# Where a step computes the scores of an attention tail and the product with U

## The chip, the cores and the metric

The kernel runs on one core of a Trainium2 chip. The metric is the time of one execution on the device in microseconds (us), the median of several executions. A profiled execution adds a trace: the start and end of every instruction on the engines PE (matrix products; PEld is its loading of weights), DVE (vector), ACT (scalar), POOL and SP, what each waited for, and every DMA.

## The reference

Everything is float32. For each of 8 batches and 8 heads there are 576 rows of queries, keys and values, 64 wide. Each row of scores keeps its 32 largest entries:

```
scores = q @ k.T / sqrt(64)              # 576 x 576 for each head
kth    = the 32nd largest of each row
attn   = softmax(where(scores >= kth, scores, -1e9))
x      = attn @ v                        # heads side by side: 8 x 576 x 512
h      = x.T @ U @ V                     # U 576 x 32, V 32 x 576: mixes the 576 rows
u      = x + h.T
out    = u + relu(u @ w_ch1) @ w_ch2     # 512 -> 2048 -> 512
```

## The kernel before

**Pairs and steps.** Two heads are one pair (`g`, 32 of them, 4 in a batch). The 576 rows of a pair are four tiles of 128 rows (`t` = 0 to 3) and a tail of 64 rows (`t` = 4, `NT`). A tile holds both heads side by side. The tail's 64 rows of one head lie on partitions 0 to 63 and those of the other on 64 to 127, so that the two heads' tails fill one tile. The list `steps` gives the first four pairs five steps each. From pair 4 on a pair has four steps, and the last of them holds two items, tile 3 and the tail: `steps += [[(g, t)] for t in range(NT - 1)] + [[(g, NT - 1), (g, NT)]]`. There are 132 steps.

**The pipeline.** The main loop counts `n` over the steps, and in one turn it works on several of them. It starts with the weighted sums of values of step n-3 (`weighted`, which calls `values`), goes on to the scores of step n+1 (`scores`, `fold`), turns the probabilities of steps n-1 and n-2 for use as a matmul operand (`turned`, `blocks`, `back`), and between these moves the top-32 search of step n (`front`) forward on DVE. `fill` is called eight times in a turn. Each call advances the generator `mixed` by one stage if one is in `mixing`, and then issues matmuls of the channel MLP of an earlier batch (`mlp`, lines 707 and 725) until a share `due` is used up. Nothing is reordered later: every engine runs its instructions in the order in which this loop issues them.

**Scores.** `scores(g, t)` multiplies queries by keys, 64 deep, into PSUM tiles `sc` (two of them, each two banks of 512 columns) and copies them to SBUF with ACT (line 361, or 368 to 370 for the first pairs). A tile takes two PSUM tiles, 288 of 512 columns in each bank, and four products of 288 columns. Each head uses one half of the PE's rows and all 128 columns (64\*128 in the trace). From pair 5 on (`blocked`) DVE later reads the first of the two PSUM tiles once more (`split`, line 400), to fold the row in two by a maximum. The tail has its own branch (`if t == NT`, lines 343 to 353): one PSUM tile, four products with 288 columns for the two heads (five where the keys of one head are stored in a rotated order), each in one quarter of the PE (64\*64), and one ACT copy into `Stail` (line 352). From pair 4 on the loop calls it at the end of the turn before the one that scores tile 3 (lines 1210 and 1211). `Stail` is first read by DVE a turn and a half later (line 468).

**Values.** `values(g, t)` multiplies probabilities by values into a PSUM tile `O`: lines 616 and 619, the latter eight products that use half of the PE's columns each (128\*64). For a tail it is line 603. ACT copies `O` into `XT` (line 628).

**The mixing with U and V.** When the tail of a pair is done, `weighted` puts `mixed(g, 5, 1 ...)` into `mixing`. One `fill` later this turns `XT` into `X` (line 642, an ACT copy, and a division by the softmax sums on POOL, line 647), then lets five `fill`s pass. The product with U follows: five products that use a quarter of the PE's columns each (line 653, `pT`, 128\*32), copied by ACT into `Tb` (line 661). The next two `fill`s multiply by V and add X (lines 665 and 667, `up`) into `uT`, the input of the MLP. With a batch's fourth pair the MLP of that batch is put into the queue `fillers`. The MLP of the last batch (`closing`, line 801) runs when all else is done.

Of the kernel before, what the change touches and what calls it, by code (L numbers as in the profile page):

```python
# [8 lines left out]
F32 = mybir.dt.float32  # L9
# [17 lines left out]
def kernel(  # L27
# [28 lines left out]
    nc = tc.nc  # L56
    B, H, S, D = q.shape
    P = 128
# [4 lines left out]
    NT, TAIL = 4, 64  # L63
    MAIN = NT * P
    HALF = S // 2
    assert S == MAIN + TAIL and D == 64 and H % 2 == 0 and C == 512 and TOPK % 8 == 0
    NPAIR = H // 2
# [15 lines left out]
    attn = ctx.enter_context(tc.tile_pool(name="attn", bufs=2))  # L83
# [43 lines left out]
    def rows(t):  # L127
        return P if t < NT else TAIL

    def cols(t):  # L130
        return slice(t * P, t * P + rows(t))
# [4 lines left out]
    def half(h):  # L136
        return slice(h * D, (h + 1) * D)
# [97 lines left out]
    raw, qkTs, S2s, uTs, XTs, dens = {}, {}, {}, {}, {}, {}  # L235
    probs, PTs, folds, fronts_of = {}, {}, {}, {}
# [54 lines left out]
    def blocked(g):  # L291

        return g > NPAIR
# [23 lines left out]
            copy(qkT[:, i, 0:MAIN], tp.rearrange("p t n -> p (t n)"))  # L319
            yield  # L320

    def scores(g, t):

        qkT = qkTs[g]
        if t == NT and g >= NPAIR:
            S2 = attn.tile([P, S], F32, tag="Stail", name="Stail", bufs=1)
        else:
            S2 = attn.tile([P, 2 * (S + TAIL)], F32, tag="Ssb", name="Ssb", bufs=4)  # L330
        n = 2 if t < NT else 1
        probs[g, t] = S2
        S2s[g, t] = S2[:, 0 : n * S].rearrange("p (c n) -> p c n", c=n)
        def product(out, h, lo, hi):
            nc.tensor.matmul(  # L335
                out,
                lhsT=qkT[half(h), 0, cols(t)],
                rhs=qkT[half(h), 1, lo:hi],
                start=True,
                stop=True,  # L340
            )

        if t == NT:
            sc = ps_s.tile([P, 2, 512], F32, tag="sc", name="sc")
            for i in range(2):
                for h in range(2):
                    lo = i * HALF + (TAIL if h and blocked(g) else 0)
                    hi = min(lo + HALF, S)
                    product(sc[half(h), i, 0 : hi - lo], h, lo, hi)
                    if hi - lo < HALF:  # L350
                        product(sc[half(h), i, hi - lo : HALF], h, 0, TAIL)
            nc.scalar.copy(S2[:, 0:S].rearrange("p (i n) -> p i n", i=2), sc[:, :, 0:HALF])
            return
        scs = [ps_s.tile([P, 2, 512], F32, tag="sc", name="sc") for _ in range(2)]
        for i, sc in enumerate(scs):
            for h in range(2):
                part = 1 - i if h and blocked(g) else i
                product(sc[:, h, 0:HALF], h, part * HALF, (part + 1) * HALF)
        if blocked(g):
            for i, sc in enumerate(scs):  # L360
                nc.scalar.copy(ends_of(S2, i), sc[:, :, 0:HALF])  # L361
            fronts_of[g, t] = scs[0][:, :, 0:HALF]
            return

        main = S2.rearrange("p (h n) -> p h n", h=2)
        last = S2[:, MAIN : MAIN + 2 * TAIL].rearrange("p (h n) -> p h n", h=2)
        copy = nc.vector.tensor_copy if g + t == 0 else nc.scalar.copy
        copy(main[:, :, 0:HALF], scs[0][:, :, 0:HALF])  # L368
        nc.scalar.copy(main[:, :, HALF:MAIN], scs[1][:, :, 0 : MAIN - HALF])
        nc.scalar.copy(last, scs[1][:, :, MAIN - HALF : HALF])  # L370

    def ends_of(S2, i):

        parts = S2[:, 0 : 4 * HALF].rearrange("p (a n) -> p a n", a=4)
        return parts[:, 1:3] if i else parts[:, 0:4:3]
# [217 lines left out]
    def values(g, t):  # L593

        PT = PTs.pop((g, t))
        va, vd, vt = (a[g % NV] for a in (vas, vds, vts))
        O = ps_t.tile([P, P], F32, tag="tp", name="O")
        if t == NT:
            den, x = dens[g], xs[g % 2]
            if g not in inverted:  # L600
                inverse(g, 2 * NT if g == NPAIR - 1 else 0, 2 * NT + 1)
            for j in range(NT + 1):
                nc.tensor.matmul(  # L603
                    O,
                    lhsT=PT[:, j],
                    rhs=va[:, :, j, :] if j < NT else vt,
                    start=(j == 0),
                    stop=(j == NT),
                )
            for h in range(2):  # L610
                nc.scalar.mul(x[half(h), NT, half(h)], O[half(h), half(h)], den[half(h), 2 * NT :])
            return
        if shared(g, t):
            PT = PT.rearrange("p c n -> p (c n)")
            PT = PT.rearrange("p (a c j) -> p c a j", a=4, j=BLK)
        nc.tensor.matmul(O, lhsT=vd, rhs=PT[:, 2 * NT], start=True, stop=False)  # L616
        for j in range(NT):
            for h in range(2):
                nc.tensor.matmul(  # L619
                    O[half(h)],  # L620
                    lhsT=va[:, h, j, :],
                    rhs=PT[:, NT * h + j],
                    start=False,
                    stop=(j == NT - 1),
                )
        if t == 0:
            XTs[g] = attn.tile([P, MAIN], F32, tag="XT", name="XT", bufs=1)
        nc.scalar.copy(XTs[g][:, cols(t)], O)  # L628


    def mixed(g, wait, lag=0):

        for _ in range(lag):
            yield
        b, gi = divmod(g, NPAIR)
        if gi == 0:
            uTs[b] = mlpp.tile([P, NC, S], F32, tag="uT", name="uT")
        XT, den = XTs.pop(g), dens[g]
        X = xs[g % 2]
        tp = ps_t.tile([P, NT, P], F32, tag="tp", name="tp")  # L640
        for t in range(NT):
            nc.tensor.transpose(tp[:, t, :], XT[:, cols(t)], ident)
        X4 = X[:, 0:NT, :].rearrange("p t (h d) -> p t h d", h=2)
        tp4 = tp.rearrange("p t (h d) -> p t h d", h=2)
        den4 = den[:, 0 : 2 * NT].rearrange("p (t h) -> p t h ()", h=2).to_broadcast([P, NT, 2, D])
        nc.scalar.copy(X4, tp4)
        nc.gpsimd.tensor_tensor(X4, X4, den4, ALU.mult)
        for _ in range(wait):
            yield
        pT = ps_t.tile([P, P], F32, tag="tp", name="pT")  # L650
        for t in range(NT + 1):
            i = t % NT * R
            nc.tensor.matmul(
                pT[i : i + R, :],
                lhsT=U[:, t, :],
                rhs=X[:, t, :],
                start=(t < NT),
                stop=(0 < t),
            )
        Tb = mlpp.tile([P, P], F32, tag="Tb", name="Tb")  # L660
        nc.scalar.copy(Tb, pT)
        yield
        for chunks, (lo, hi) in zip(PARTS, SPAN):
            up = ps_t.tile([P, WIDE], F32, tag="tp", name="up")
            nc.tensor.matmul(up[:, 0 : hi - lo], lhsT=Tb, rhs=V[:, lo:hi], start=True, stop=False)  # L665
            for t in chunks:
                nc.tensor.matmul(  # L667
                    up[:, OFF[t] - lo : OFF[t] - lo + rows(t)],
                    lhsT=X[:, t, :],
                    rhs=ident if t < NT else ident2,  # L670
                    is_transpose=True if t < NT else None,
                    start=False,
                    stop=(t == chunks[-1]),
                )
            nc.scalar.copy(uTs[b][:, gi, lo:hi], up[:, 0 : hi - lo])
            yield
        if gi == NPAIR - 1:
            fillers.append(closing(b) if b == B - 1 else mlp(b))

    posts, ticks = [], 0  # L680

    def later(wait, job):

# [338 lines left out]
    STEPS = len(steps)  # L1022
# [5 lines left out]
    fillers, mixing, due = [], [], 0.0  # L1028
# [21 lines left out]
    def tiles(n):  # L1050

        return steps[n] if 0 <= n < STEPS else []

    def weighted(m):

        for g, t in reversed(tiles(m)):
            values(g, t)
        if tiles(m)[-1][1] == NT:
            mixing.append(mixed(g, 5, 1 if m < STEPS - 1 else 0))

    def turn():

# [10 lines left out]
    t = 0  # L1073
    for _ in prep(0):
        pass
    scores(0, 0)
    turning = ready = iter(())
    fronts = {}
    for n in range(STEPS + 2):
        if n < STEPS:  # L1080
            g, t = steps[n][0]
# [6 lines left out]
        else:  # L1088
            t = NT
# [71 lines left out]
        fill()  # L1161
        if ALONE <= n - 3 <= STEPS - 3:
            weighted(n - 3)
        for tile_ in tiles(n + 1):
            if tile_[1] < NT:
                scores(*tile_)
            fold(*tile_)
        turn()
        fill()
# [37 lines left out]
            next_params(1)  # L1207
        next(here, None)
        fill()
        if len(tiles(n + 2)) > 1:  # L1210
            scores(*tiles(n + 2)[1])
        fill()
    while mixing or fillers:
        fill()
# [33 lines left out]
```

## Time and profile before

| | |
|---|---|
| median of 3 executions | 1689.52 us (1689.05 to 1690.55) |
| profiled execution | 1690.17 us |
| its span, first to last instruction | 1688.4 us |
| PE busy | 1597.7 us (95%), 9328 matmuls |
| DVE busy | 1544.0 us (91%) |
| ACT busy | 1001.9 us (59%) |
| POOL busy | 938.1 us (56%) |
| PE in 500 to 1500 us | no idle time in the record |
| scores of a tail with 64 rows of the PE and 64 columns | 32 times, first at 35.6 us, last at 1513.2 us |
| product with U | 32 times, first at 87.1 us, last at 1563.9 us |

The span is 1.8 us below the profiled execution's own time and 1.1 us below the median. A float32 matmul of the program is two records in the trace, each with its load of weights. The record of a matmul [...]overlaps the next one, so the cost of a matmul is read from the distance between starts, not from its duration. Counts such as x10 are counts of records.

### The profile page before, as it was taken

The numbers are of one execution on the slowest core, as the hardware profiler recorded it, in microseconds if no ns is written. First come the engines' busy times: TensorE is split into PE (matmuls) and PEld (weight loads), VectorE is DVE, ScalarE is ACT, GpSimd is POOL, SyncE is SP. The second block draws the span as 40 slices with busy tenths as digits, with TensorE's granted clock in tenths as the row PEclk, the third lists the DMA queues.
The fourth block names the chain that finished last, engine by engine and source line by source line (L and its number), as shares of the span: only waits on it lengthen the run. The fifth ranks groups of instructions, "written<-read, shape, count | busy, mean of one in ns | idle before, by whom it ended". The sixth has DMA issues, their size and how long they took to land.

```text
span 1688.4 us, 29105 instructions
## 1 busy us (share of the span) xinstructions
PE 1597.7 (95%) x9328; PEld 1202.3 (71%) x9328; DVE 1544.0 (91%) x4364; ACT 1001.9 (59%) x2447; POOL 938.1 (56%) x741
## 2 busy tenths in 40 slices
PE   4667799999999999999999999999999999999999
PEld 2444566788677877778777887778777887778876
DVE  7999998999999999999999999999999999994452
ACT  4888778665555556565665556565655656564320
POOL 4778668655555555555555555555555555553620
PEclk7787798999999999999999999999999999999999
DMA  3323232254545545454444545454445455443001
GB/s 87 97 77 93 59 89 72 59 134 122 126 115 134 125 126 135 122 133 119 126 116 129 125 130 124 124 129 127 122 114 129 124 134 126 126 116 102 10 1 29
DMA packets 273897, 180.96 MB, mean 107 GB/s; under 512 B 171376, under 2 KB 258256, under 8 KB 273744
## 3 DMA queue, kind: packets, MB, share of 16 engines
q1 hardware_dynamic: 257712, 117.49, 30.1%
q10 hardware_dynamic: 16032, 61.61, 11.3%
q8 instruction: 74, 1.21, 0.3%
q14 instruction: 79, 0.65, 0.1%
HBM read 108.23 MB, written 70.78 MB: 106 GB/s over the span
## 4 chain that ended last, share of the span: by engine, by line
PE 82%; DVE 14%; ACT 1%; issue 1%; POOL 1%; DMA 1%; SPq 0%; ACTq 0%; DVEq 0%; POOLq 0%
PE mm L725 26%; PE mm L707 24%; PE sc L335 9%; PE O L619 7%; DVE m L486 6%; DVE upper L481 5%; PE mm L801 3%; PE up L665 2%; DVE first L468 2%; PE O L603 2%; PE tp L801 2%; PE sc L801 2%; PE O L616 1%; PE tp L578 1%; PE up L667 1%; PE tp L749 1%
## 5 line engine op out<-in xcount | busy, mean ns | idle before, releaser
L516 POOL TENSOR_TENSOR Ssb<-Ssb,E 128x576 f32<-128x576 f32 x243 | 339.6, 1417 | 273.7 <-ACT E L515 273.5
L707 PE MATMUL mm<-uT,w 128*128 128x320 f32 (+1 forms) x1792 | 468.7, 412 | 0.3 <-ACT hT L720 0.3
L725 PE MATMUL mm<-hT,w 128*128 128x320 f32 (+1 forms) x1792 | 468.0, 410 | 0.0
L707 PEld LDWEIGHTS mm<-uT,w 128*128 128x128 f32 x1792 | 331.6, 191 | 96.9 <-issue 9.0
L725 PEld LDWEIGHTS mm<-hT,w 128*128 128x128 f32 x1792 | 328.8, 190 | 90.7 <-issue 12.7
L486 DVE MAX8 m<-upper 128x8 f32<-128x304 f32 (+1 forms) x780 | 366.5, 510 | 0.7
L481 DVE MATCH_REPLACE8 upper<-m,upper 128x304 f32<-128x304 f32 (+1 forms) x520 | 259.3, 505 | 0.0
L398 POOL TENSOR_TENSOR lower<-Ssb 128x576 uint32<-128x576 uint32 x108 | 152.5, 1412 | 153.4 <-issue 102.2
L335 PE MATMUL sc<-qkT 64*128 64x288 f32 (+1 forms) x1334 | 213.1, 442 | 11.3 <-ACT Ssb L368 7.8
L405 ACT ACTIVATE Ssb<-Ssb,nmax 128x576 f32<-128x576 f32 x258 | 200.9, 780 | 17.4 <-POOL Ssb L492 9.2
L401 POOL TENSOR_TENSOR lower<-lower,upper 128x576 uint32<-128x576 uint32 x108 | 152.6, 1413 | 103.6 <-DVE upper L400 99.9
L453 DVE MAX8 upper<-lower 128x8 f32<-128x288 f32 x432 | 171.9, 438 | 9.8 <-POOL lower L401 9.7
L515 ACT ACTIVATE E<-Ssb,least 128x576 f32<-128x576 f32 x243 | 176.2, 768 | 4.3
L335 PEld LDWEIGHTS sc<-qkT 64*128 64x128 f32 (+1 forms) x1334 | 116.7, 184 | 74.5 <-issue 30.5
L542 DVE STREAM_TRANSPOSE y<-Ssb 128x512 f32<-128x512 f32 (+1 forms) x312 | 154.5, 544 | 7.0 <-ACT Ssb L405 6.4
L720 ACT ACTIVATE hT<-mm 128x320 f32<-128x320 f32 (+1 forms) x224 | 91.2, 407 | 100.8 <-PE mm L707 96.4
L361 ACT COPY Ssb<-sc 128x576 f32<-128x576 f32 x216 | 127.7, 644 | 37.0 <-PE sc L335 37.0
L619 PE MATMUL O<-PT,va 128*64 128x128 f32 x2048 | 145.1, 286 | 0.0
L619 PEld LDWEIGHTS O<-PT,va 128*64 128x64 f32 x2048 | 113.8, 141 | 16.4 <-issue 2.0
L400 DVE TENSOR_TENSOR upper<-sc,Ssb 128x576 f32<-128x576 f32 x108 | 80.1, 742 | 21.8 <-ACT Ssb L361 21.8
L628 ACT COPY XT<-O 128x128 f32<-128x128 f32 x128 | 33.9, 265 | 107.1 <-PE O L619 106.9
L481 DVE MATCH_REPLACE8 upper<-first,upper 128x304 f32<-128x304 f32 x216 | 97.4, 458 | 0.0
(247 smaller groups left out, 2191.6 us busy)
## 6 DMA issues: line engine op xcount, KB each, us to landing
away<-y SPq DMA_DIRECT2D x416, 144.0 KB, 2.5
PT<-away ACTq DMA_DIRECT2D x104, 576.0 KB, 3.8
raw<-in_moe_w_ch_dram SPq DMA_DIRECT2D x32, 512.0 KB, 3.8
va<-in_v_dram SPq DMA_DIRECT2D x64, 128.0 KB, 2.4
out_dram<-ob SPq DMA_DIRECT2D x59, 128.0 KB, 2.0
ld<-in_q_dram SPq DMA_DIRECT2D x108, 64.0 KB, 2.6
ld<-in_k_dram SPq DMA_DIRECT2D x108, 64.0 KB, 2.5
ld<-in_q_dram SPq DMA_DIRECT2D x108, 8.0 KB, 2.9
```

The lines of the kernel that those rows point to most:

```text
L335: nc.tensor.matmul(out, lhsT=qkT[half(h), 0, cols(t)], rhs=qkT[half(h), 1, lo:hi], start=True, stop=True,)
L401: nc.gpsimd.tensor_tensor(bottom, bottom, top.bitcast(U32), ALU.subtract)
L405: nc.scalar.activation(E, chunk, AF.Exp, bias=nmax, scale=SCALE, accum_out=total)
L453: nc.vector.max(spot, lower)
L481: nc.vector.match_replace(nxt, ms[c], curs[c], NEG)
L486: nc.vector.max(ms[c], curs[c])
L515: nc.scalar.activation(gap, chunk, AF.Relu, bias=least[:, c : c + 1], scale=-WIDEN)
L516: nc.gpsimd.tensor_tensor(chunk, chunk, gap, ALU.subtract)
L542: nc.vector.transpose(y[:, :, i * NT : i * NT + c].rearrange("p r c j -> p c r j"), E2[:, a : a + c * P].rearrange("p (c r j) -> p c r j", ...
L619: nc.tensor.matmul(O[half(h)], lhsT=va[:, h, j, :], rhs=PT[:, NT * h + j], start=False, stop=(j == NT - 1),)
L707: nc.tensor.matmul(ph[:, 0:w], lhsT=first_layer(cc, f), rhs=uT[:, cc, lo:hi], start=(cc == 0), stop=(cc == NC - 1),)
L725: nc.tensor.matmul(po[:, 0:w], lhsT=w2[:, f, c * P : (c + 1) * P], rhs=hTs[f][:, 0:w], start=(f == 0), stop=(f == NF - 1),)
```

## The change

Two pieces of work get other places in a turn, from pair 4 on.

The tail's scores are no longer computed at the end of a turn but by the call of `scores` that computes tile 3, ahead of tile 3's own products. They have no PSUM tile of their own: they go in three parts of 192 columns into columns 288 to 479 of three of the four banks that tile 3's scores use. The third part crosses the end of the first 512 keys and is computed in two pieces, so there are eight products (four of 192, two of 128, two of 64 columns). A new function copies them into `Stail` with two ACT copies (384 and 192 columns) after the copies of tile 3.

The product with U, for pairs 4 to 30, no longer follows after five `fill`s. `mixed` puts its pair into a new list `waiting` and stands still until the list is cleared. The main loop clears it in the next turn, right after the weighted values and ahead of the scores, and takes that one stage of `mixed` forward. The two stages with V follow at the next two `fill`s. The last pair keeps its five `fill`s. One variant of a buffer for tails of the first pairs is simplified and does the same as before.

```diff
-    def scores(g, t):
+    def scores(g, t, tail=False):
         qkT = qkTs[g]
-        if t == NT and g >= NPAIR:
-            S2 = attn.tile([P, S], F32, tag="Stail", name="Stail", bufs=1)
-        else:
-            S2 = attn.tile([P, 2 * (S + TAIL)], F32, tag="Ssb", name="Ssb", bufs=4)
+        S2 = attn.tile([P, 2 * (S + TAIL)], F32, tag="Ssb", name="Ssb", bufs=4)
...
         scs = [ps_s.tile([P, 2, 512], F32, tag="sc", name="sc") for _ in range(2)]
+        third = S // 3
+        spots = [sc[:, i, HALF : HALF + third] for sc, i in ((scs[0], 0), (scs[0], 1), (scs[1], 0))]
+        if tail:
+            rows_ = slice(MAIN, S)
+            for i, spot in enumerate(spots):
+                for h in range(2):
+                    lo, hi = i * third, min((i + 1) * third, MAIN)
+                    first_ = TAIL if h and blocked(g) else 0
+                    ranges = [(0, lo + first_, hi + first_)]
+                    if (i + 1) * third > MAIN:
+                        ranges.append((hi - lo, 0 if first_ else MAIN, TAIL if first_ else S))
+                    for to, lo, hi in ranges:
+                        nc.tensor.matmul(
+                            spot[half(h), to : to + hi - lo],
+                            lhsT=qkT[half(h), 0, rows_],
+                            rhs=qkT[half(h), 1, lo:hi],
+                            start=True,
+                            stop=True,
+                        )
...
             fronts_of[g, t] = scs[0][:, :, 0:HALF]
+            if tail:
+                tail_copies(g, scs, third)
             return
...
+    def tail_copies(g, scs, third):
+        S2 = attn.tile([P, S], F32, tag="Stail", name="Stail", bufs=1)
+        probs[g, NT] = S2
+        S2s[g, NT] = S2.rearrange("p (c n) -> p c n", c=1)
+        nc.scalar.copy(
+            S2[:, 0 : 2 * third].rearrange("p (i n) -> p i n", i=2), scs[0][:, :, HALF : HALF + third]
+        )
+        nc.scalar.copy(S2[:, 2 * third : S], scs[1][:, 0, HALF : HALF + third])
...
         nc.gpsimd.tensor_tensor(X4, X4, den4, ALU.mult)
-        for _ in range(wait):
-            yield
+        if wait is None:
+            waiting.append(g)
+            while g in waiting:
+                yield
+        else:
+            for _ in range(wait):
+                yield
         pT = ps_t.tile([P, P], F32, tag="tp", name="pT")
...
-            mixing.append(mixed(g, 5, 1 if m < STEPS - 1 else 0))
+            mixing.append(mixed(g, None, 1) if m < STEPS - 1 else mixed(g, 5, 0))
...
             weighted(n - 3)
+            if waiting:
+                waiting.clear()
+                if next(mixing[0], True):
+                    mixing.pop(0)
         for tile_ in tiles(n + 1):
             if tile_[1] < NT:
-                scores(*tile_)
+                scores(*tile_, len(tiles(n + 1)) > 1)
             fold(*tile_)
...
         fill()
-        if len(tiles(n + 2)) > 1:
-            scores(*tiles(n + 2)[1])
         fill()
```

More of the change, by code (lines that the diff above doesn't have):

```diff
@@ L370, in scores @@
         nc.scalar.copy(last, scs[1][:, :, MAIN - HALF : HALF])
+        if tail:
+            tail_copies(g, scs, third)
+    def tail_copies(g, scs, third):
[6 more added lines that the diff above has]
+        nc.scalar.copy(S2[:, 2 * third : S], scs[1][:, 0, HALF : HALF + third])
     def ends_of(S2, i):
@@ L678, in mixed @@
             fillers.append(closing(b) if b == B - 1 else mlp(b))
-    posts, ticks = [], 0
+    posts, ticks, waiting = [], 0, []
     def later(wait, job):
```

## The prediction

> **What bounds the kernel now.** I read the chain of work that ended last first. The line gives each engine's share of the span:
>
> ```profile
> PE 82%; DVE 14%; ACT 1%; issue 1%; POOL 1%; DMA 1%; SPq 0%; ACTq 0%; DVEq 0%; POOLq 0%
> ```
>
> PE carries the end. Where, is told by the busy times in stretches (columns: stretch, length, busy of PE, PEld, DVE, ACT, POOL with counts, granted PE clock, DMA share, GB/s):
>
> ```profile
> 432.00:1530.00 1098.00, 1097.66 (x6537) 831.60 (x6533) 1069.08 (x3230) 655.95 (x1612) 601.76 (x458) 1.00 0.49 125
> 266.00:432.00 166.00, 162.13 (x1023) 125.50 (x1021) 157.67 (x476) 108.95 (x267) 107.35 (x83) 0.98 0.40 98
> ```
>
> From 432 to 1530 us PE has no idle time and DVE has 29 us of it. A busy PE need not be a PE at its pitch, so I ask the waits for what PE stands on after 432 us:
>
> ```profile
> PE tp L1003 <- DVE oT L981: 0.5, 1, 0.5
> PE mm L707 <- ACT hT L720: 0.3, 1, 0.3
> PE O L616 <- DMA PT<-away: 0.3, 1, 0.3
> ```
>
> 1.1 us in all. PE's own issue sets this stretch, and only what shortens it pays. The timeline of PE around one tail shows what an issue costs (start, length, line, use of the PE as rows\*columns, shape, records):
>
> ```profile
> 838.54 5.55 PE L707 MATMUL mm<-uT,w 128*128 128x320 f32 x20
> 844.02 1.20 PE L335 MATMUL sc<-qkT 64*64 64x288 f32 x10
> 845.14 1.88 PE L707 MATMUL mm<-uT,w 128*128 128x320 f32 x6
> 846.86 1.05 PE L603 MATMUL O<-va,PTt 128*128 128x128 f32 x8
> ...
> 848.29 1.09 PE L619 MATMUL O<-PT,va 128*64 128x128 f32 x16
> 849.32 1.24 PE L335 MATMUL sc<-qkT 64*128 64x288 f32 x8
> 850.49 1.35 PE L707 MATMUL mm<-uT,w 128*128 128x320 f32 x4
> 851.67 0.60 PE L642 MATMUL tp<-ident,XT 128*128 128x128 f32 x4
> 852.11 4.47 PE L707 MATMUL mm<-uT,w 128*128 128x320 f32 x16
> 856.51 0.62 PE L653 MATMUL pT<-x,U 128*32 128x128 f32 x10
> 857.06 1.34 PE L707 MATMUL mm<-uT,w 128*128 128x320 f32 x4
> 858.24 0.70 PE L665 MATMUL up<-V,Tb 128*128 128x320 f32 x2
> ```
>
> Undisturbed, a record of 320 columns takes 0.269 us (24 of L707 from 816.98 to 823.44 us, same view, other window). Twenty of them should take 5.38 us; the tail starts 5.48 after the first. So 0.10 is lost on leaving the full array. The tail takes 1.12 us. The next six should take 1.61 and take 1.72: 0.11 more is lost on coming back. The product with U shows the same: 16 records take 4.40 instead of 4.30, the product 0.55, and the four after it 1.18 instead of 1.08. Each excursion costs its work and 0.20 us besides. Values (L619) and scores (L335, 64\*128) already stand side by side, in two other uses of the array.
>
> **What the Trainium skill says.** "TensorEngine Tiling (Array Packing)", Key Properties: changing the tiling mode drains the TensorE. The 0.09 to 0.10 us at every change above agrees. "TensorE: Matmul & The Clock Gate", LDWEIGHTS: a load costs its columns / 1.2 in ns, 107 ns for 128. That fits the 0.10 to 0.11 us of the first full matmul after a change, whose load starts with it instead of ahead of it; at the tail's own start, with 64 columns, the first distance is 0.29 us against 0.24 for the next. The same page, Part 1, says that PE's clock halves after an idle window of some 3.4 us; here it was 0.50 from 425.6 to 432.4 us, after PE had waited 2.95. "PSUM — Partial Sum Buffer", PSUM bank collisions, says that two engines must not be on one bank and quadrant at once, ACT and DVE included. That bears on the new copies, below; no row of before shows it.
>
> **The change part by part.**
>
> *Tail's scores, 28 times (pairs 4 to 31).* Before: 0.10 + 1.12 + 0.11 = 1.33 us between MLP matmuls. The 1.12 holds its first load (0.05) and the drain after it (0.09), so 0.98 of products; one head's 576 columns, twice, at 0.84 ns (0.269 / 320) are 0.97. After: the order of the changed program is values, tail, tile 3's scores. The drain after values and the exposed load of the scores are paid already. Added are the tail's first load, its products and the drain after it: 1.12, if the products still take 0.98. Saved: 0.21.
>
> The products are eight now: 192 + 192 + 128 + 64 columns for each head, the same sum, and the heads run side by side in two quarters. But the third part is issued as 128, 64 of the first head, then 128, 64 of the second. If PE starts the second head only once the first is through, that costs up to 2 x 192 x 0.84 = 0.32 us. If it doesn't, nothing. I take nothing: in the product with U four column groups start within 0.02 us (records at 856.508 to 856.528), though each has a second record that has to wait for its own first, so PE passes waiting records of other tiles, three of them there as here. Changing from 64\*64 to 64\*128 may need no drain or load exposure, as the rows stay split: another gain of up to 0.20. No row shows this change; I take the full cost.
>
> *Product with U, 27 times (pairs 4 to 30).* Before 0.10 + 0.55 + 0.11 = 0.76; after, between values and scores, 0.55. Saved: 0.21. I use 0.20 for both, as the trace's hundredths allow.
>
> *Where it counts.* Tails start at 220, 274, 324, 369 and 414 us and then 23 times more; of the products with U, four lie before 432 and 23 after. 46 x 0.20 = 9.2 us after 432. Before 432 DVE is the pace (157.7 of 166 us) and PE waits once, so the 9 savings there count as nothing; at most 1.8.
>
> *The one stall.* At 421.9 us the MLP queue is empty and PE waits 2.95 us for POOL's X (L647), then runs at half clock. After the change the values stand ahead of the product with U there, and need a transfer (PT<-away) issued at 422.18 that takes 3.8 us in the median, 4.9 there. PE resumes near 426.5 instead of 425.0. At the durations of before at half clock, values 2.6, product 1.1, scores 2.1, then the two `up` 0.9 and 0.75 put the first MLP matmul at 434.0 against 433.4: a loss of 0.6. It could be a gain of 3 if PE wakes sooner, or a loss of 2 if the half clock holds for one more window.
>
> *DVE.* Its order is unchanged. Its fold (L400) now waits in the program for the first tail copy too, one bank being read by both: 0.47 us of ACT (576 columns take 0.64, 320 0.42). That sets DVE back in phase once per pair, not in rate: it has no more work. Its room is this wait,
>
> ```profile
> DVE upper L400 <- ACT Ssb L361: 18.9, 20, 1.6
> ```
>
> 18.9 us between 432 and 1530, against 9.2 that PE gains. POOL keeps its instructions.
>
> *ACT.* Two copies (0.47 + 0.32) for one (0.64), moved behind tile 3's copies; `Tb` moves ahead of them. ACT is 60% busy there. The `up` product waits for `Tb`, which used to be covered by two MLP matmuls (1.08 us) and now by tile 3's-kind scores (1.17). SP and its queue: some output transfers trade places with `away` transfers, none is added.
>
> *Sum.* 1688.4 - 9.2 + 0.6 = 1679.8 us of span; some 0.3 of the last savings are lost to the transfer that PE meets at 1546.8 us (the 0.3 in the waits). With the 1.1 us between span and median: 1681.2.
>
> **The rivals.**
>
> *The third part runs one head after the other.* For it: the issue order, and the skill's statement (same TensorE page, Part 3) that matmuls keep program order; against it, the records of U's product. Price 0.22 to 0.32 x 23 = 5 to 7.4 us; the time is 1686 to 1689.
>
> *DVE becomes the bound.* For it: 97% busy, and nearly no waits from 340 to 480 us. Against: 18.9 us of waits, spread over the batches at 1 to 2 us a pair, where PE gains 0.4. Gain cut to some 3 us: 1686.5.
>
> *No drain between tail and scores.* 23 x 0.1 to 0.2 = 2 to 4.6 more: 1677 to 1679.
>
> *Slower: `up` waits for `Tb` at every product with U.* If ACT is inside its pair of Relu passes (L515, 1.44 us) when values end, `XT` and `Tb` (0.27 each) come up to 2.0 us after them, later still where L515 waits on DVE; PE, which gets to `up` 1.8 us after them (0.55 + 1.17 + a drain), then stands. Nothing is behind it on PE but the MLP. It decides from 0.4 us a pair on; at 0.6 it makes 23 x 0.6 = 13.8 less 8.3: 1695. Against it:
>
> ```profile
> ACT XT L628 <- PE O L619: 106.9, 94, 2.5
> ```
>
> ACT waited for the values in 94 of 128 cases, 1.1 us each, so it is ready.
>
> **How the numbers follow.** Main case 0.60 (1679 to 1684 with the stall's uncertainty); no drain 0.11; one head after the other 0.13; DVE 0.07; slower 0.09. This kernel's measurement tells 0.2% (3.4 us) from no change. Under 1686.1 are the main case, no drain, and half of the serial case: 0.78. Within: the rest of the serial case and DVE: 0.13. Slower: 0.09. The range from 1676 to 1688 leaves out the slower case and the far ends of others.
>
> **What would show it.** Right: PE without idle time after 432; the tail's row takes 1.12 us and its MLP neighbours meet without the 0.21; the same around U's product; waits of DVE at the fold down by about half; the count of matmul records up by 170 (27 x 6 + 8). Wrong: a tail block of 1.35 us or more (serial), new waits of PE on `Tb` or `sc`, a longer stall near 422 us.

## The result: 1685.82 us, less than half of the gain that was forecast

The changed kernel takes 1685.82 us in the median of 10 executions (1684.42 to 1687.68), the kernel before 1689.70 us beside it (1688.86 to 1690.55). The ratio is 0.9976, its 95% interval 0.9967 to 0.9986, so the gain is 2.4 to 5.6 us, 3.9 in the middle. The sign and the range of the forecast hold; its size, 8.3 us, does not.

The profiled execution has a span of 1684.5 us, 3.9 below before, so the trace can be used to find the missing part. The line of the chain of work that ended last, after the change:

```profile
PE 54%; DVE 32%; SPq 4%; DMA 4%; issue 2%; POOL 2%; ACT 1%; DVEq 0%; ACTq 0%; POOLq 0%
```

PE had 82% of that chain, DVE 14. Now the chain leaves PE at some place and goes through a transfer, SP's queue and DVE. The busy times in the same two stretches (length, busy of PE, PEld, DVE, ACT, POOL with counts, granted clock, DMA share, GB/s):

```profile
432.00:1530.00 1098.00, 1095.79 (x6715) 846.79 (x6712) 1074.56 (x3244) 657.28 (x1645) 603.15 (x458) 1.00 0.50 125
266.00:432.00 166.00, 160.08 (x1043) 125.91 (x1039) 157.79 (x477) 108.58 (x269) 107.17 (x83) 0.98 0.40 98
```

DVE is busy 5.5 us more from 432 to 1530 us, as more of its work falls into the stretch (3244 instructions instead of 3230); PE now has 2.2 us without work, where it had 0.3. What PE stands on after 432 us (the waits of PE):

```profile
PE mm L742 <- ACT hT L755: 1.9, 2, 1.5
PE O L646 <- DMA PT<-away: 1.6, 1, 1.6
PE tp L1038 <- DVE oT L1016: 0.6, 1, 0.6
PE up L700 <- ACT Tb L696: 0.4, 1, 0.4
```

4.5 us in all against 1.1. (The MLP's lines 707, 720 and 725 are 742, 755 and 760 now, values 616 and 619 are 646 and 649, the product with U is 688, the tail 364, `up` 700.) The two moved pieces in the timeline of PE, around the same pair as in the prediction:

```profile
844.80 1.09 PE L649 MATMUL O<-PT,va 128*64 128x128 f32 x16
845.83 1.25 PE L364 MATMUL sc<-qkT 64*64 64x192 f32 x16
847.01 1.24 PE L332 MATMUL sc<-qkT 64*128 64x288 f32 x8
...
856.57 1.09 PE L649 MATMUL O<-PT,va 128*64 128x128 f32 x16
857.60 0.62 PE L688 MATMUL pT<-x,U 128*32 128x128 f32 x10
858.15 1.24 PE L332 MATMUL sc<-qkT 64*128 64x288 f32 x8
```

The product with U takes 0.55 us, as before and as forecast. The tail's block takes 1.18 us (845.83 to 847.01), not 1.12: neither of the forecast's main case nor of its serial rival (1.35 or more).

**How far ahead PE is.** The start of the same tile's scores in both traces gives PE's lead, place by place. Three such places, before and then after:

```profile
549.97 1.24 PE L335 MATMUL sc<-qkT 64*128 64x288 f32 x8
...
1314.93 1.24 PE L335 MATMUL sc<-qkT 64*128 64x288 f32 x8
...
1518.63 1.24 PE L335 MATMUL sc<-qkT 64*128 64x288 f32 x8
```

```profile
549.63 1.24 PE L332 MATMUL sc<-qkT 64*128 64x288 f32 x8
...
1309.15 1.24 PE L332 MATMUL sc<-qkT 64*128 64x288 f32 x8
...
1512.60 1.24 PE L332 MATMUL sc<-qkT 64*128 64x288 f32 x8
```

Between the first and the second (16 pairs) the lead grows from 0.34 to 5.78 us, 0.340 us a pair. At both places the changed kernel has issued six MLP records fewer than the kernel before, so this growth is at equal work. All through this stretch the change pays, at a steady rate. At the last scores the lead is 6.03 us. But behind them 188 matmul records of the batch's MLP are still to come, in the kernel before 184: two matmuls, four records of 0.216 us (24 such records took 5.18 us in the run with credit, below), 0.86 us, had been put off. At equal work the lead is 5.17 us. The end comes only 3.9 us sooner. The rows that tell of the last loss, of before and of after (timeline of PE; in brackets its idle time ahead of the row and what ended it):

```profile
1546.79 0.46 PE L616 MATMUL O<-PT,vd 128*128 128x128 f32 x2 [0.29 <-DMA PT<-away]
```

```profile
1523.96 0.81 PE L700 MATMUL up<-V,Tb 128*128 128x320 f32 x2 [0.36 <-ACT Tb L696]
1541.86 0.46 PE L646 MATMUL O<-PT,vd 128*128 128x128 f32 x2 [1.60 <-DMA PT<-away]
```

At 1541.86 us PE waits 1.31 us longer than it did for the transposed probabilities of the last tile 3, and 5.17 - 1.31 is 3.86. So the question is threefold: why the lead at the last scores is 5.2 and not 9, what is lost before the steady stretch and after it, and what the last wait is.

### The profile page after: what moved, and what is told of

Same layout as the page of the kernel before. It is cut to its first block, busy times and chain, and to the rows that moved or that the text cites. A ratio compares the mean times of both kernels' runs of the same rounds, so it can differ in the third digit from the quotient of the medians.

```text
span 1684.5 us, 29512 instructions
## 1 busy us (share of the span) xinstructions
PE 1586.0 (94%) x9498; PEld 1213.4 (72%) x9498; DVE 1543.7 (92%) x4364; ACT 1000.1 (59%) x2475; POOL 939.0 (56%) x741
## 4 chain that ended last, share of the span: by engine, by line
PE 54%; DVE 32%; SPq 4%; DMA 4%; issue 2%; POOL 2%; ACT 1%; DVEq 0%; ACTq 0%; POOLq 0%
PE mm L760 16%; PE mm L742 16%; DVE m L516 10%; DVE upper L511 9%; PE sc L332 4%; PE O L649 4%; DVE first L498 3%; PE mm L836 3%; DVE y L572 3%; DVE upper L483 2%; PE sc L836 2%; PE tp L836 2%; DVE place L511 2%; DMA ld<-in_k_dram 2%; SPq L255 2%
## 5 line engine op out<-in xcount | busy, mean ns | idle before, releaser
L742 PE MATMUL mm<-uT,w 128*128 128x320 f32 (+1 forms) x1792 | 461.1, 410 | 1.9 <-ACT hT L755 1.9
L760 PE MATMUL mm<-hT,w 128*128 128x320 f32 (+1 forms) x1792 | 461.5, 408 | 0.0
L332 PE MATMUL sc<-qkT 64*128 64x288 f32 (+1 forms) x1056 | 178.8, 460 | 10.8 <-ACT Ssb L386 7.8
L332 PEld LDWEIGHTS sc<-qkT 64*128 64x128 f32 (+1 forms) x1056 | 95.7, 197 | 51.2 <-issue 16.4
L481 DVE MATCH_REPLACE8 lower<-upper,lower 128x288 f32<-128x288 f32 x216 | 94.1, 444 | 0.0
```

The costliest lines, as they stand in the source:

```text
L332: nc.tensor.matmul(out, lhsT=qkT[half(h), 0, cols(t)], rhs=qkT[half(h), 1, lo:hi], start=True, stop=True,)
L742: nc.tensor.matmul(ph[:, 0:w], lhsT=first_layer(cc, f), rhs=uT[:, cc, lo:hi], start=(cc == 0), stop=(cc == NC - 1),)
L760: nc.tensor.matmul(po[:, 0:w], lhsT=w2[:, f, c * P : (c + 1) * P], rhs=hTs[f][:, 0:w], start=(f == 0), stop=(f == NF - 1),)
```

## The experiments

Two theories stand against each other at the start. *Two places*: the savings are real in mid-run, and what is missing is lost at the turn near 422 us, where the MLP has no work left, and at the end. *DVE's rate*: each fold now waits for a tail copy, DVE has become the bound, and one of the two moves is worth nothing.

### One move alone

Only the tail is moved; the product with U keeps its five fills:

```diff
-            mixing.append(mixed(g, None, 1) if m < STEPS - 1 else mixed(g, 5, 0))
+            mixing.append(mixed(g, 5 if g in range(NPAIR, NP) else None, 1) if m < STEPS - 1 else mixed(g, 5, 0))
```

> Only the tail's scores and products are moved; the product with U keeps its five fills. Theory (the savings are real on PE in mid-run, and are lost at two places, the dry turn near 422 us and the end): 23 tails after 432 us save 0.15 us each, 3.4 us; the dry turn is as before, since the product with U of pair 7 is not moved, so two MLP matmuls are not displaced; at the end the fold of the last pair waits for the tail's first copy, which costs 1 to 2 us. 1687.0 to 1688.5 us. Rival 1 (DVE sets the rate all along, because every fold waits for a tail copy): nothing is gained, 1689.5 us or more, and the change's whole gain is that of the product with U. Rival 2 (the third part runs one head after the other): a tail block of 1.35 us, no saving, 1690 us.

Measured: 1688.77 us beside 1690.47 for before, ratio 0.9989 (0.9983 to 0.9996).

Only the product with U is moved; the tail stays at the end of a turn, with its own PSUM tile (this and the later edits that put a tail back also give it its old buffer `Stail`; that hunk is left out):

```diff
-                scores(*tile_, len(tiles(n + 1)) > 1)
+                scores(*tile_, len(tiles(n + 1)) > 1 and tile_[0] not in range(NPAIR, NP))
...
+        if len(tiles(n + 2)) > 1 and tiles(n + 2)[1][0] in range(NPAIR, NP):
+            scores(*tiles(n + 2)[1])
```

> Only the product with U is moved; the tail's scores and products stay at the end of the step. Theory of the two places: 23 products save 0.20 us each, 4.5 us; the dry turn costs 0.6 for the longer stall and 0.9 for two MLP matmuls that come at the end instead; the last-but-one pair's wait for Tb costs 0.4. 1686.7 to 1687.7 us. Rival 1 (the loss is the tail copies' alone): 1685.2 us, faster than with both moves.

Measured: 1688.02 us, ratio 0.9988 (0.9982 to 0.9995).

Both times are 0.3 us above the upper end of what was expected. Each move gives about half, which goes against one of them being eaten by DVE. The traces are sharper: in the 16 pairs from 550 to 1315 us the tail alone gains 2.27 us, 0.142 a pair, and the product with U 3.17 us (0.46 to 3.63), 0.198 a pair. Together 0.340, the rate of both moves, to the last digit. A DVE that set the rate would break this sum. DVE's own waits agree: of the 18.9 us at the fold in 432 to 1530 us, this is left after the change,

```profile
DVE upper L430 <- ACT Stail L397: 9.1, 16, 1.0
```

about half, as forecast, and not used up.

With the tail alone the lead is 1.10 us at the scores that stood at 454.23 us before, -0.14 at those of 466.84, 0.00 at 514.58, 0.14 at 562.4 and 2.98 at the last. So each of the 23 tails behind 460 us pays its 0.142 (the first is already in the -0.14), and what was saved ahead of 460 us is lost there, with 0.28 us besides. Where it goes, that trace shows in these rows: PE in the turn near 422 us, then PE and ACT near 460 us.

```profile
424.86 1.06 PE L688 MATMUL pT<-x,U 128*32 128x128 f32 x10 [3.10 <-POOL x L677]
...
460.01 3.50 PE L742 MATMUL mm<-uT,w 128*128 128x320 f32 x12 [1.18 <-ACT hT L755]
```

```profile
459.15 0.33 ACTq L587 DMA_DIRECT2D PT<-away  x1
459.52 0.44 ACT L755 ACTIVATE hT<-mm 128x320 f32<-128x320 f32 x1 [2.59 <-DMA away<-y]
```

ACT issues the transfer `PT<-away` and has to wait for the four transfers `away<-y`, which DVE's transposes feed. A Relu of the MLP is queued behind that issue on ACT, and PE needs the Relu's PSUM bank. The Trainium skill says that ACT's queue is a strict FIFO ("TensorE: Matmul & The Clock Gate", Architectural detail); this stall of 2.59 us on ACT and of 1.18 us on PE is what that costs here.

It is not DVE that takes the lead here. The last of the four `away<-y` is issued at 454.98 us, 1.17 us sooner than before (456.15), but takes 4.10 us to land where it took 2.64, and so lands 0.28 us later than before (459.08 against 458.80). The line on the four of them in 452 to 462 us, its last number their median time to landing, before and with the tail alone:

```profile
away<-y SPq DMA_DIRECT2D x4, 144.0 KB, 2.5
```

```profile
away<-y SPq DMA_DIRECT2D x4, 144.0 KB, 3.4
```

### The last pair's tail in its old place

```diff
-                scores(*tile_, len(tiles(n + 1)) > 1)
+                scores(*tile_, len(tiles(n + 1)) > 1 and tile_[0] not in (NP - 1,))
...
+        if len(tiles(n + 2)) > 1 and tiles(n + 2)[1][0] in (NP - 1,):
+            scores(*tiles(n + 2)[1])
```

> Both moves, but the last pair's tail keeps its old place, so that its copies do not stand ahead of the last fold. Theory of the two places, if the loss at the end is from the late fold of the last pair: the saving of one tail is given up (0.15) and 0.5 to 1.5 us of the end come back, 1684.5 to 1685.5 us. Rival (the end's loss was already there in the pairs before, as ACT's and DVE's delay): 1685.9 to 1686.2 us, no gain.

Measured: 1685.51 us, ratio 0.9972 (0.9962 to 0.9983), not to be told from the changed kernel. In its trace the wait at the last tile 3 is 1.36 us instead of 1.60: some 0.2 us, less than expected. The late tail copies are a small part of the end's loss.

### Pair 7's product with U in its old place

```diff
-            mixing.append(mixed(g, None, 1) if m < STEPS - 1 else mixed(g, 5, 0))
+            mixing.append(mixed(g, 5 if g in (2 * NPAIR - 1,) else None, 1) if m < STEPS - 1 else mixed(g, 5, 0))
```

> Both moves, but the product with U of pair 7, the one in the turn where the MLP queue is dry near 422 us, keeps its five fills. Theory of the two places: one saving given up (0.20), the stall as before (0.6 back), no MLP matmul displaced (0.9 back): 1684.4 to 1684.9 us, and MLP matmuls after the last scores 92 again. Rival (what happens at 422 us is made up for later): 1685.8 to 1686.2 us.

Measured: 1684.77 us, ratio 0.9969 (0.9957 to 0.9980). The time is as expected, but within the interval of the changed kernel's, so that what follows here and in the next two experiments rests on the traces; the reason given is only half right. The rows of the turn and its sequel, before and in the changed kernel:

```profile
425.00 0.62 PE L653 MATMUL pT<-x,U 128*32 128x128 f32 x10 [2.95 <-POOL x L647]
...
449.88 3.07 PE L707 MATMUL mm<-uT,w 128*128 128x320 f32 x10 [0.34 <-ACT hT L720]
```

```profile
426.72 0.77 PE L646 MATMUL O<-PT,vd 128*128 128x128 f32 x2 [3.89 <-DMA PT<-away]
...
449.53 4.14 PE L742 MATMUL mm<-uT,w 128*128 128x320 f32 x14 [1.45 <-ACT hT L755]
```

The wait of 3.89 us and the half clock after it were forecast (a longer stall here was also named as a sign of being wrong). The half clock before came after a wait of 2.95 us, shorter than the window of some 3.4 us that the prediction cites. That PE then meets a late Relu at 449.5 us (0.34 us before, 1.45 now) was not. With pair 7's product put back the stall is 3.10 us and the wait at 449.5 us is gone, but one of 1.22 comes near 460 us, as with the tail alone. In the middle, at the scores that were at 1457.93 us, PE's lead is 7.84 us against 7.12.

Why the Relu is late, ACT's rows tell, before and in the changed kernel. Each shows the fourth Relu of that batch's MLP and the DMA issue near it:

```profile
446.65 0.42 ACT L720 ACTIVATE hT<-mm 128x320 f32<-128x320 f32 x1
...
449.02 0.33 ACTq L557 DMA_DIRECT2D PT<-away  x1
```

```profile
448.67 0.33 ACTq L587 DMA_DIRECT2D PT<-away  x1
449.04 0.44 ACT L755 ACTIVATE hT<-mm 128x320 f32<-128x320 f32 x1 [0.66 <-DMA away<-y]
```

Before, the Relu stands ahead of the issue in ACT's order; now, with two MLP matmuls fewer issued by the scores that stood at 443.6 us, it stands behind it. It is so in every kernel in which pair 7's product is moved, and PE waits 1.3 to 2.1 us there; in all others this Relu runs at 445.1 to 446.8 us, and PE waits at most 0.3 us. No run moves that Relu by itself.

The 92 matmuls that were expected behind the last scores did not come back: there are 94. The trace shows why. Two MLP matmuls are dropped not at 422 us but between the scores that stood at 623.0 and 635.9 us before, one batch on. `fill` sets its credit to zero when the queue is empty (`if not fillers: due = 0.0`), and the moved product, hence the next batch's MLP, comes a turn's part later than it did. Each kernel with the product moved loses two matmuls of credit once: at the first batch boundary where the product is late. No further loss shows in the counts; the backlog of two that stays in the queue would explain it.

### The lost credit given back after the last scores

```diff
     for n in range(STEPS + 2):
+        if n == STEPS:
+            due += 1.6
```

> Both moves, and after the last scores the fills are given 1.6 more of credit, so that the two MLP matmuls which the turn at 422 us lost are issued ahead of the values near 1542 us instead of after them. Theory (PE's wait there, 1.60 us against 0.29 before, is the hole that these two matmuls, 0.86 us, left): the wait falls to 0.75 us and the end comes 0.86 us sooner, 1684.9 us, span 1683.6. Rival (the wait is DVE's lateness alone and moves with PE): the wait stays near 1.6, 1685.6 to 1686.0 us.

Measured: 1684.65 us, ratio 0.9970 (0.9959 to 0.9981), span 1683.1. The row at the last tile 3, where PE waited 1.60 us:

```profile
1541.55 0.46 PE L646 MATMUL O<-PT,vd 128*128 128x128 f32 x2 [0.67 <-DMA PT<-away]
```

0.93 us of the wait is gone, by two matmuls worth 0.86: they had left a hole. Of the 1.31 us by which the wait grew, 0.4 is left: PE has become earlier by more than the transfer that it waits for, which DVE feeds. The run with the last tail back puts 0.2 of this down to the tail copies.

### Seven products a tail

The first head's third part does not wrap round and can be one product:

```diff
-                    if (i + 1) * third > MAIN:
+                    if (i + 1) * third > MAIN and not first_:
+                        ranges = [(0, lo, S)]
+                    elif (i + 1) * third > MAIN:
                         ranges.append(
```

> Both moves, but the first head's third part, which doesn't wrap round, is one product of 192 columns instead of 128 and 64: seven products a tail instead of eight. Theory (the tail's block is 1.18 us instead of 1.12 because it has four more products): the block takes 1.16 to 1.17, 22 times 0.015 is 0.3 us: 1685.5 us. Rival (it is the order of the third part, one head partly behind the other): the block falls to 1.12 or less, 22 times 0.06 is 1.3 us: 1684.5 us. Rival (it is the way into the scores): 1.18 stays, 1685.8 us.

Measured: 1684.10 us, ratio 0.9967 (0.9955 to 0.9980). The tail's block in its trace:

```profile
845.23 1.20 PE L366 MATMUL sc<-qkT 64*64 64x192 f32 x14
846.36 1.24 PE L332 MATMUL sc<-qkT 64*128 64x288 f32 x8
```

1.13 us instead of 1.18: one product less takes back nearly all that eight had cost over the old tail's 1.12. That is the second theory's number, and it speaks against a cost of the size that was expected for each product. The single records show something of the order: with eight products the first head's 128 columns run as records from 846.530 and 846.639 us, the second head's from 846.537 and 846.696, 0.057 after the first head's where elsewhere in the block it is 0.007. (The trace does not name the heads; records only 0.007 us apart are taken as one of each, since one head's own follow each other by 0.11 us or more.) So the second head was held, but by 0.05 us, not by the 0.11 to 0.16 us a record (128 to 192 columns at 0.84 ns) that one head after the other would take. Nor do the products start in program order: the first head's 64 columns, issued ahead of the second head's 128, start 0.21 us after them, at 846.748. The skill's sentence that matmuls keep program order (the same TensorE page, Part 3), on which the serial rival leaned, does not hold here. What in the array holds the second head for 0.05 us stays open. From 550 to 1315 us the gain is 0.370 a pair instead of 0.340, somewhat less than the block's 0.05.

### Both moves for pairs 4 to 7 alone

```diff
-            mixing.append(mixed(g, None, 1) if m < STEPS - 1 else mixed(g, 5, 0))
+            mixing.append(mixed(g, 5 if g in range(2 * NPAIR, NP) else None, 1) if m < STEPS - 1 else mixed(g, 5, 0))
...
-                scores(*tile_, len(tiles(n + 1)) > 1)
+                scores(*tile_, len(tiles(n + 1)) > 1 and tile_[0] not in range(2 * NPAIR, NP))
...
+        if len(tiles(n + 2)) > 1 and tiles(n + 2)[1][0] in range(2 * NPAIR, NP):
+            scores(*tiles(n + 2)[1])
```

> Both moves for pairs 4 to 7 alone; from pair 8 on everything stands as before. Theory (savings ahead of 432 us are absorbed by DVE's pace, and the turn at 422 us costs 1.0 to 1.4 us): slower than before by 0.5 to 1.5 us, 1690.9 to 1691.9 us against the 1690.4 that before showed on the last chip, and d of +0.9 to +1.4 us at equal work from 456 us on. Rival (nine early savings count): faster than before by 0.5 to 1.5 us.

Measured: 1692.05 us beside 1689.57, ratio 1.0014 (1.0008 to 1.0021): 1.4 to 3.5 us slower. The theory has the sign and is short in size. The early part of the change costs time by itself, and the trace has it at both places, 1100 us apart:

```profile
426.72 0.76 PE L649 MATMUL O<-PT,vd 128*128 128x128 f32 x2 [4.75 <-DMA PT<-away]
449.31 4.14 PE L745 MATMUL mm<-uT,w 128*128 128x320 f32 x14 [1.27 <-ACT hT L758]
...
1547.92 0.46 PE L649 MATMUL O<-PT,vd 128*128 128x128 f32 x2 [1.30 <-DMA PT<-away]
```

At equal work PE is 1.4 us behind at the last scores. The wait at the last tile 3 is 1.30 us, although from pair 8 on every tail and every product stands as before: 1.0 us more than before, for two matmuls put off at 422 us. The tail alone is faster than before, and pair 7's product put back gave lead, so it is most likely the turn at pair 7 that costs; no run moves that product alone.

### All four edits joined, and the seventh product with pair 7's alone

Joined: pair 7's and pair 30's product with U at five fills, the last pair's tail in its old place, the credit, and seven products (the last as edited above).

```diff
-            mixing.append(mixed(g, None, 1) if m < STEPS - 1 else mixed(g, 5, 0))
+            mixing.append(mixed(g, 5 if g in (2 * NPAIR - 1, NP - 2) else None, 1) if m < STEPS - 1 else mixed(g, 5, 0))
...
+        if n == STEPS:
+            due += 1.6
...
-                scores(*tile_, len(tiles(n + 1)) > 1)
+                scores(*tile_, len(tiles(n + 1)) > 1 and tile_[0] not in (NP - 1,))
...
+        if len(tiles(n + 2)) > 1 and tiles(n + 2)[1][0] in (NP - 1,):
+            scores(*tiles(n + 2)[1])
```

> Both moves, with pair 7's and pair 30's product with U left at five fills, the last pair's tail in its old place, the 1.6 of credit after the last scores and seven products a tail. Theory (the losses lie at the turn at 422 us and at the end): the turn gives 1.2 back, the end 1.0 to 1.5, the seventh product 0.3, less 0.7 of savings given up or already counted: 1682.8 to 1684.0 us, below the changed kernel by 2 to 3 us. Rival (DVE is the bound by the end, whatever PE has saved): 1684.6 us, as with pair 7's product alone left behind.

Measured: 1681.40 us (1680.39 to 1683.20), ratio 0.9954 (0.9940 to 0.9967), span 1678.6. It is below both kernels, and better than expected; its interval only touches the changed kernel's, at 0.9967. What PE waited for after 432 us:

```profile
PE tp L1043 <- DVE oT L1021: 0.6, 1, 0.6
PE O L651 <- DMA PT<-away: 0.5, 1, 0.5
PE mm L747 <- ACT hT L760: 0.3, 1, 0.3
```

1.4 us in all, about the 1.1 of before. The wait for a Relu near 450 to 460 us is down to 0.3. To see whether that was this run's fortune or came with one of the edits, the joined kernel ran again, with one that has only the seven products, edited as above, and pair 7's product at five fills:

```diff
-            mixing.append(mixed(g, None, 1) if m < STEPS - 1 else mixed(g, 5, 0))
+            mixing.append(mixed(g, 5 if g in (2 * NPAIR - 1,) else None, 1) if m < STEPS - 1 else mixed(g, 5, 0))
```

> Both moves, pair 7's product with U left at five fills, seven products a tail; no credit, the last pair's tail in its new place. Theory (the parts of the joined kernel add up): 1684.8 less 1.0 to 1.5 for the seventh product, 1683.3 to 1683.8 us, and one wait of PE of 1.2 us for hT near 460 us as in the kernel with pair 7's product alone left behind. Rival (the two together keep PE from that wait, which gave the joined kernel 2.5 us from 479 us on): 1681.5 to 1682.5 us, no wait at 460 us.

> The joined kernel once more, for its time and a second profile. Theory (its lead of 2.9 us at 479 us is its own): 1681 to 1682 us, the lead at 479 us is 2.5 to 3 us again. Rival (it was a fortunate start of that run): 1682.5 to 1683.5 us, and PE waits for hT near 450 to 460 us.

Measured, on one chip beside 1689.46 us for before: 1682.14 us (1681.63 to 1682.88), ratio 0.9957 (0.9943 to 0.9970), with seven products and pair 7 alone, and 1681.86 us (1680.72 to 1682.51), ratio 0.9954 (0.9942 to 0.9967), for the joined kernel. PE's wait for a Relu after 432 us in the former:

```profile
PE mm L744 <- ACT hT L757: 0.2, 1, 0.2
```

The rival holds for the first: no stop at 460 us, and 1682.1. For the joined kernel neither holds whole: its time came back, but its lead at 479 us was 1.28 us this time instead of 2.89, without the wait for a Relu that the rival had named. So 1.6 us of the lead at that place differ between two profiles of one kernel. The stop at 450 to 460 us is what all three profiles of the kernels with both edits lack. Where PE stopped at 460 us (tail alone, pair 7 back), the transfers `away<-y` in 452 to 462 us took 3.4 us in the median, in those three and in the kernel before 2.5. Why they do is not settled, nor whether it comes with these kernels or with single executions.

### The changed kernel once more

> The changed kernel once more, for a second profile: PE's wait of 0.40 us for hT at 1494 us, which neither the change's parts nor the kernel with credit showed. Theory (it is left over from the start of the run, where transfers fall differently each time): the stretch from 1484 to 1512 us shows no wait of PE, the values near 1542 us still wait 1.3 to 1.6 us, and the mid-run differences are the same to 0.05 us. Rival (it belongs to the change): the wait is there again.

No edit; one execution, 1685.79 us, span 1684.0. The second of the two waits for a Relu in the first profile, 0.40 us at 1494 us, with which PE's lead fell back by 0.8 us, is absent, so it does not belong to the change (in the other kernels the lead falls there by 0.3 and 0.4 us in two traces, and not in the rest). But the wait at the last tile 3 is 1.87 us instead of 1.60, at the upper end and beyond what was expected: a PE that comes 0.75 us earlier gets only 0.5 us of it at that point, where it waits for the transfer.

**All runs in one table.** The lead is taken at the last scores at equal work (0.86 us less where two MLP matmuls are put off); its difference from the growth of the last wait over 0.29 us should be the gain of the span.

| kernel | lead, us | last wait, us | lead less growth of wait | gain of the span |
|---|---|---|---|---|
| changed | 5.17 | 1.60 | 3.9 | 3.9 |
| changed, second profile | 5.93 | 1.87 | 4.3 | 4.4 |
| tail alone | 2.98 | 0.84 | 2.4 | 2.5 |
| product with U alone | 3.13 | 1.02 | 2.4 | 2.4 |
| last tail back | 5.43 | 1.36 | 4.4 | 4.4 |
| pair 7 back | 6.40 | 1.33 | 5.4 | 5.4 |
| credit | 5.85 | 0.67 | 5.5 | 5.3 |
| seven products | 7.02 | 1.53 | 5.8 | 5.8 |
| pairs 4 to 7 alone | -1.41 | 1.30 | -2.4 | -2.2 |
| seven, pair 7 back | 9.18 | 1.40 | 8.1 | 8.1 |
| joined | 10.02 | 0.54 | 9.8 | 9.8 |
| joined again | 8.50 | 0.46 | 8.3 | 8.3 |

Two numbers read from a trace give every span to 0.2 us: nothing more than that is lost at another place behind the last scores.

## Why the prediction was wrong

The mechanism was right: PE's issue sets the mid-run, each excursion from the full array costs 0.2 us besides its work, and placing it between two others saves most or all of that (0.14 and 0.20). The sum was not. The forecast was 9.2 for 46 savings, less 0.6 for the turn and 0.3 for the end. The first profile has 7.6 by the last scores (23 tails of 0.142, 22 products with U of 0.198), less 1.6 near the turn, 0.8 at 1494 us and 1.3 at the end: 3.9. What was missing in the forecast is a change in the fillers' order: two MLP matmuls are put off. That costs at the end, as the run with credit shows, and by the traces at the turn too.

*"Tail's scores ... Saved: 0.21."* Measured 0.142 (0.198 for the product with U). "I take nothing" for the third part was wrong by 0.05 us: the second head is held for a moment. Against the 0.20 that the sum used for both, the pair's 0.340 is 0.060 short, 1.4 us over 23 pairs. The product of pair 30, also counted, comes after the last scores, where no scores follow it. The serial rival had the right place and four to six times the size. *No drain between tail and scores* fell too: the last 64-column record of the tail starts at 846.861 and the scores 0.148 later, as it was 0.148 from the old tail to the MLP.

*"Where it counts."* The count of 23 tails held, by the leads of the tail alone. That the savings ahead of 432 us count as nothing is not shown. DVE is as busy there after the change (157.8 of 166 us), but with the tail alone 1.10 us of lead had come through the turn, and a slow transfer near 460 us took it.

*"The one stall."* 0.6 was put down for the turn near 422 us. At the scores that stood at 466.84 us before, the changed kernel's lead is -0.42 us, and four MLP records of 0.269 us (1.08) are put off; pair 9's tail had already saved 0.14. So 1.6 us are lost by then. Other kernels tell how much of this goes with pair 7's product. In the mid-run lead, putting it back is worth 0.7 us over the changed kernel though it gives up a saving of 0.2, so moving it costs 0.9; between the two kernels with seven products the leads at 1457.93 us are 10.21 and 8.06 us, so there it costs 2.4. (With pair 7 back, the kernel with eight products stops near 460 us, and the one with seven does not.) What failed is that the step ended with the first MLP matmul at 434 us: its start was right (434.31), but the Relu that had moved behind a DMA issue on ACT held PE again, 1.45 us at 449.5. The 0.8 us at 1494 us were lost in the first profile and not in the second.

*"Some 0.3 of the last savings are lost to the transfer that PE meets at 1546.8 us."* This is the term that was most out of size, 1.31 (1.58 in the second profile). 0.9 of it comes from a step that the forecast did not have: the fills drop their credit when the queue is dry, and two MLP matmuls that would have covered the wait came after it. The moves were counted, the change in the fillers' order was not. The other 0.4 is the forecast's own 0.3, about as large as forecast: PE gains, the transfer fed by DVE follows late.

*"That sets DVE back in phase once per pair, not in rate"* held, by the slopes that add up and the 9.1 us of waits left. *DVE becomes the bound* gave the right time (1686.5) for the wrong reason. *`up` waits for `Tb`* happened once after 432 us, 0.36 us at pair 30, where no scores follow to cover it; it decides nothing at one pair.

## What to carry to other kernels

When an engine that is full is made faster, look up the two places where it is not full, the start and the end of its stretch: there a saving can be taken back by a wait for a transfer. Work that fills gaps by a credit moves when anything else does. If the credit is dropped on an empty queue, a late event can move a result behind a wait on another engine soon after, and leave a hole at the end hundreds of microseconds later. A DMA issue on ACT's queue that waited for another transfer held all that was behind it, so a compute result that a third engine waits for should not stand there.

## What the runs showed that was not expected

Products in different quarters of the array overtook each other: a product of the second head started 0.21 us ahead of one of the first head that was issued before it. Splitting a 192-column product in two (128 and 64) cost 0.05 us of the block, though the columns are the same. The traces agree in mid-run to 0.1 us between runs of one kernel (the lead's growth from 550 to 1315 us was 5.44 in both profiles of the changed kernel, 7.45 and 7.54 in those of the joined one). The lead at 550 us differed by 0.1 us between the former two and by 1.6 between the latter, about the 1.5 us by which the joined kernel's two spans differ.
